# Attention regrouped into runs of eight products, and an auction step with its thresholds on VectorE

## The chip, the cores and the metric

The kernel runs on one core of one Trainium2 chip. The metric is the device time of one execution in microseconds (us). A core has a matrix engine (TensorE, PE in the profile, with its weight loads as PEld), a vector engine (VectorE, DVE), a scalar engine (ScalarE, ACT), GpSimd (POOL) and SyncE (SP), which in this kernel only issues transfers. Each engine works through its own instructions in the order in which they are written; they wait for one another through semaphores.

## The reference

Three parts follow one another: a sigmoid attention, a mixture of experts whose tokens are assigned greedily under a capacity, and a dense layer pair with a squared activation. Cut to what matters:

```
scores = q @ k.T / sqrt(64) - log(448)            # 4 batches, 12 heads, 448 x 64
x = sigmoid(scores) @ v                           # -> 1792 tokens x 768
logits = x @ w_gate                               # 1792 x 8 experts
for idx in argsort(-logits.flatten()):            # best (token, expert) first
    if token is free and expert has < 224 tokens: assign
h = relu(x[mask] @ w1[e]); y[mask] = h @ w2[e]     # per expert, 768 -> 1024 -> 768
r = relu(y @ w_in); out = (s * r * r + b) @ w_out  # 768 -> 2048 -> 768
```

## The kernel before

The program has a schedule written out by hand: what stands first in the source is issued first on its engine.

**Attention.** There are 24 pairs (4 batches b, 6 pairs of heads p). For a pair the scores come in four chunks of 112 keys (`NC = 4`). A score chunk is two products (tile psc, one head each, side by side on TensorE), followed by one sigmoid on ScalarE into attn. A value chunk is two products into pv, summed over the four chunks; then ScalarE copies pv to xT. In `scores_av(n, i, mid)` two score chunks of pair n = i + 1 alternate with two value chunks of pair i, so TensorE changes between score products and value products after every four products. psc has two buffers, pv two. The trace counts two records for each such product. Through the callback `mid` the gate's products are put between these groups: `gate` (logits of a batch, tile plg), `gate_copy`, `gate_turn` (to tokens by experts, tile pt), `gate_last` (the last pair of the last batch, which needs its xT). `prefs` on VectorE then ranks a batch's logits; `bracket`, in three stages during the last batch, finds the range for the first threshold.

Beside this, 32 blocks of the dense weights are converted from 64 bit to 32 bit (`convert`, on VectorE): craw is loaded, four VectorE instructions make co, and co is written to nw. `CONV[i]` says how many follow pair i. SyncE issues, in this order for pair i, vt of pair i + 2, rk and rq of pair i + 3, then the writes and loads of the conversions. `w_dma`, `w_high` and `w_low` prepare the first expert weights (the last on GpSimd here).

**Auction.** The assignment is found by a parallel search of ten steps. An array of 128 lines holds (chunk of tokens, expert), 112 tokens wide. A step claims with the present threshold (`choose`: VectorE aw, TensorE pa), takes out lost tokens (VectorE LM), counts at ten thresholds (six compares on VectorE, three sign passes on ScalarE, counted into cnt), sums the counts on TensorE (pb), and takes from them the new threshold (jd, into dv) and the factor for the next step size (jf, into cut). From the second step on, GpSimd makes the step sizes (dv) and thresholds (th) from dv, cut and least. In the same steps TensorE turns x to token rows (`rows_in`: four transposes into px for one of 24 rows), ScalarE copies px to xrow, and a transfer writes xrow to xs in HBM; `ROWS` says how many rows go with each step. The first four transfers are issued by ScalarE, the others by SyncE.

**Places and experts.** `places` turns the claims into row numbers idx: one-hot rows oh on VectorE, 32 small products on TensorE (pi), two copies and two sums. GpSimd then gathers the first expert's rows from xs; `keep_clock` puts idle products on TensorE meanwhile. The experts and the dense layers follow and fill the rest of the program.

Of the kernel before, what the change touches and what calls it, by code (L numbers as in the profile page):

```python
# [8 lines left out]
F32 = mybir.dt.float32  # L9
# [15 lines left out]
CP = 112  # L25
# [14 lines left out]
WARM = (9, 10)  # L40
ROWS = (2, 2, 2, 3, 3, 3, 2, 2, 2, 2)
SYNC = 4
SIGNS = 2
CONV = [1, 1, 2, 1, 2] * 4 + [1, 2, 1]
FULL = CAP - 0.5
# [16 lines left out]
def tile_kernel(ctx, tc, qT, kT, v, wg, w1, w2, wi, wo, s2, b2, cst, out):  # L62
# [55 lines left out]
    att = ExitStack()  # L118
    qk = att.enter_context(tc.tile_pool(name="qk", bufs=4))
    vp = att.enter_context(tc.tile_pool(name="vp", bufs=2))  # L120
    at = att.enter_context(tc.tile_pool(name="at", bufs=2))
    ps_s = att.enter_context(tc.tile_pool(name="ps_s", bufs=2, space=PSUM))
    ps_v = att.enter_context(tc.tile_pool(name="ps_v", bufs=2, space=PSUM))
    ps_l = att.enter_context(tc.tile_pool(name="ps_l", bufs=1, space=PSUM))
# [22 lines left out]
    def convert():  # L147
        if not coming:
            return
        i = coming.pop(0)  # L150
        r = craw.pop(i)
        lo, hi = r[:, :, 0], r[:, :, 1]
        b = cgp.tile([128, 768], I32, name="cb_", bufs=2)
        a = cgp.tile([128, 768], I32, name="co", bufs=3)
        V.tensor_scalar(a, hi, 3, 0x3FFFFFFF, op0=ALU.logical_shift_left, op1=ALU.bitwise_and)
        V.tensor_scalar(b, lo.bitcast(U32), 2.0 ** -29, None, op0=ALU.mult)
        V.scalar_tensor_tensor(a, hi, -(1 << 30), a, op0=ALU.bitwise_and, op1=ALU.bitwise_or)
        V.tensor_tensor(a, a, b, op=ALU.add)
        cout.append((i, a))
        cv_out(1)  # L160
        cv_in()
# [48 lines left out]
    def load_v(i):  # L210
        b, p = pairs[i]
        vt[i] = vp.tile([CP, NC, 128], F32, name="vt", bufs=4)
        nc.sync.dma_start(vt[i], v[b, p])
# [8 lines left out]

    def scores_av(n, i, mid):
        if n is not None:
            rq, rk = raw_qk.pop(n)
            attn[n] = at.tile([CP, 2, NC, S], F32, name="attn")
        if i is not None:
            a = attn.pop(i)
            pv = ps_v.tile([128, 512], F32, name="pv")
        for c2 in range(0, NC, 2):  # L230
            for c in (c2, c2 + 1):
                mid(c)
                if n is not None:
                    p = ps_s.tile([CP, 2, 512], F32, name="psc")
                    for j in range(2):
                        me = slice(j * D, (j + 1) * D)
                        T.matmul(p[:, j, :S], rk[me, c * CP:(c + 1) * CP], rq[me], start=True, stop=True)  # L237
                    A.activation(attn[n][:, :, c, :], p[:, :, :S], AF.Sigmoid, bias=nls[:CP],  # L238
                                 scale=1.0 / math.sqrt(D))
            for c in (c2, c2 + 1):  # L240
                if i is not None:
                    for j in range(2):
                        T.matmul(pv[j * 64:(j + 1) * 64, :S], vt[i][:, c, j * D:(j + 1) * D], a[:, j, c, :],  # L243
                                 start=(c == 0), stop=(c == NC - 1))
        if i is not None:
            b, p = pairs[i]
            xt = xT[:, p, b * S:(b + 1) * S]
            if i == len(pairs) - 1:
                A.copy(xt[:, :2 * CP], pv[:, :2 * CP])
                A.copy(xt[:, 2 * CP:], pv[:, 2 * CP:S])  # L250
            else:
                A.copy(xt, pv[:, :S])

    def gate(b, p0, p1, last):
        if p0 == 0:
            plg[b] = ps_l.tile([128, 512], F32, name="plg")
        for p in range(p0, p1):
            i = p % 4
            T.matmul(plg[b][i * 32:(i + 1) * 32, :S], wgs[:, p], xT[:, p, b * S:(b + 1) * S],
                     start=(p < 4), stop=(p + 4 >= last))  # L260
# [5 lines left out]
    def gate_turn(b, stop):  # L266
        lg = lgs.pop(b)
        pt = ps_l.tile([128, 512], F32, name="pt")
        pts[b] = pt[:CP, :NC * E].rearrange("p (c e) -> p c e", e=E)
# [20 lines left out]
    def bracket(stage):  # L290
# [4 lines left out]
        elif stage == 1:  # L295
            pm = ps_l.tile([128, 512], F32, name="plg")
            T.transpose(pm[:2, :CP], mm[:CP], ident[:CP, :CP])
# [3 lines left out]
        else:  # L301
            pr = ps_l.tile([128, 512], F32, name="plg")
            T.matmul(pr[:, :2], on[:2], dg, start=True, stop=True)
# [29 lines left out]
    load_qk(2)  # L333
    cv_in()
    cv_in()
    cv_in()
    scores_av(0, None, lambda c: None)
    nc.sync.dma_start(sb2[:, 0:1], s2.partition_broadcast(128))
# [13 lines left out]
    for i in range(N):  # L352
        b, p = pairs[i]
        if i + 2 < N:
            load_v(i + 2)
        if i + 3 < N:
            load_qk(i + 3)
        def mid(c):
            if b == B - 1 and p == 5:
                if c == 0:  # L360
                    gate(b, 0, 5, 5)
                elif c == 2:
                    gate_copy(b)
                elif c == 3:
                    gate_turn(b, False)
            elif p == 5 and c == 0:
                gate(b, 0, 4, 6)
            elif p == 0 and b and c == 1:
                gate(b - 1, 4, 6, 6)
            elif p == 0 and b and c == 3:  # L370
                gate_copy(b - 1)
            elif p == 1 and b and c == 0:
                gate_turn(b - 1, True)

        scores_av(i + 1 if i + 1 < N else None, i, mid)
        if p == 1 and b:
            prefs(b - 1)
        if b == B - 1 and 2 <= p <= 4:
            bracket(p - 2)
        if N - 6 <= i < N - 2:  # L380
# [4 lines left out]
        if i < N - 1:  # L385
            for _ in range(CONV[i]):
                convert()
    gate_last(B - 1)
    prefs(B - 1)
# [31 lines left out]

    got = rows_in(1)
    pl = ps_1.tile([128, CP], F32, name="pl")
# [15 lines left out]
    def auction(n, fill):  # L439
        for it in range(n):  # L440
            if fill and it == 0:
                pv = choose(dv[0], pw)
                V.tensor_copy(WT, pw)
            else:
                pv = choose(dv[0])
# [3 lines left out]
            if it or not fill:  # L449
                G.tensor_scalar(dv[0][:, 1:], dv[1][:, 1:], cut, least, op0=ALU.mult, op1=ALU.max)  # L450
                G.tensor_scalar(th, kvec, dv[0][:, 1:2], dv[0][:, 0:1], op0=ALU.mult, op1=ALU.add)
            V.scalar_tensor_tensor(LM, pv, -BIG, LT, op0=ALU.mult, op1=ALU.min)
# [17 lines left out]
            if fill:  # L470
                if it in AHEAD:
                    w_dma()
            dv.reverse()
            V.scalar_tensor_tensor(jd, pc[:, 1:], FULL, dv[1], op0=ALU.is_ge, op1=ALU.mult,
                                   accum_out=dv[0][:, 0:1])
            V.scalar_tensor_tensor(jf, pc, FULL, fvec, op0=ALU.is_ge, op1=ALU.mult, accum_out=cut)
        settle(choose(dv[0]))

# [358 lines left out]
```

## Time and profile before

| | us |
|---|---|
| three runs | 963.48, 968.11, 972.67 |
| median | 968.11 |
| the profiled execution | 965.9 |
| its span, first to last instruction | 964.1 |

The profiled execution lies 2.2 us below the median, and 1.8 us of its time lie around the span. TensorE is busy 97% of the span, VectorE 58%, ScalarE 46%, GpSimd 14%. The span can be read in four stretches: attention to about 180 us, the auction from there to about 217 us, places and the first gather to about 228 us, and the experts and dense layers from there to the end. TensorE's granted clock is full in the first and the last stretch and half of that in most of the auction.

### The profile page before, as it was taken

What the parts mean: (1) busy time and instruction counts of PE and PEld (TensorE: products, weight loads), DVE (VectorE), ACT (ScalarE), POOL (GpSimd) and SP (SyncE); (2) the same over time, 40 slices, a digit from 0 to 9 for tenths busy, and PEclk for the clock granted to TensorE, in tenths of its full rate; (3) what the DMA queues carried; (4) which work ended last, traced back from release to release, by engine and by line L of the source; (5) the groups of instructions that cost most, each with busy time, mean ns of one, the idle gap of its engine ahead of it and who ended that gap; (6) DMA issues with size and microseconds to landing.
All of it is one profiled execution on the core that took longest, in us unless ns stands there. A gap on an engine that the chain in (4) does not pass through costs nothing.

```text
span 964.1 us, 14094 instructions
## 1 busy us (share of the span) xinstructions
PE 937.4 (97%) x5277; PEld 782.4 (81%) x5277; DVE 563.9 (58%) x1015; ACT 443.8 (46%) x771; POOL 137.4 (14%) x136
## 2 busy tenths in 40 slices
PE   9999999778999999999999999999999999999997
PEld 3333333466899999999999999999999999999997
DVE  3565635764777774278677321877774278677320
ACT  5666666573564332266533223664332266433220
POOL 1000001223330000153100002430000152100001
PEclk9999999857999999999999999999999999999999
DMA  8999996272674434477443433774434476533411
GB/s 288 380 318 360 351 374 230 98 228 79 208 232 145 124 114 137 131 244 234 142 138 108 127 99 91 262 233 147 118 116 140 131 235 204 152 121 109 119 46 66
DMA packets 68456, 173.08 MB, mean 180 GB/s; under 512 B 7968, under 2 KB 24864, under 8 KB 68384
## 3 DMA queue, kind: packets, MB, share of 16 engines
q1 hardware_dynamic: 64256, 160.22, 51.5%
q0 software_dynamic: 2272, 11.01, 3.3%
q10 hardware_dynamic: 1856, 0.92, 0.3%
q8 instruction: 42, 0.69, 0.3%
q14 instruction: 30, 0.25, 0.1%
HBM read 148.52 MB, written 23.59 MB: 179 GB/s over the span
## 4 chain that ended last, share of the span: by engine, by line
PE 82%; DVE 6%; DMA 5%; issue 3%; ACT 2%; POOL 1%; SPq 1%; POOLq 0%; ACTq 0%; DVEq 0%
PE acc L642 9%; PE acc L708 8%; PE acc L710 8%; PE acc L709 8%; PE acc L759 8%; PE acc L761 8%; PE acc L760 8%; PE pv L243 7%; PE psc L237 7%; PE acc L643 5%; DVE wl L198 2%; DMA raw<-in_w_dram 2%; DMA rq<-in_qT_dram 2%; PE px L409 2%; ACT wh L187 1%
## 5 line engine op out<-in xcount | busy, mean ns | idle before, releaser
L187 ACT CAST wh<-raw 128x768 fp32r<-128x768 f32 (+1 forms) x240 | 209.2, 878 | 160.1 <-PE acc L761 133.8
L198 DVE TENSOR_TENSOR wl<-raw,wh 128x768 fp32r<-128x768 f32 (+1 forms) x198 | 210.5, 1068 | 104.9 <-ACT wh L187 104.9
L198 POOL TENSOR_TENSOR wl<-raw,wh 128x768 fp32r<-128x768 f32 (+1 forms) x42 | 92.1, 2201 | 433.4 <-ACT wh L187 285.2
L759 PE MATMUL acc<-wh,gt 128*128 128x384 f32 x448 | 149.9, 335 | 0.0
L760 PE MATMUL acc<-wl,gt 128*128 128x384 f32 x448 | 149.7, 334 | 0.0
L761 PE MATMUL acc<-wh,gt 128*128 128x384 f32 x448 | 149.6, 334 | 0.0
L708 PE MATMUL acc<-y,wh 128*128 128x448 f32 x384 | 141.4, 368 | 0.0
L710 PE MATMUL acc<-y,wl 128*128 128x448 f32 x384 | 140.6, 366 | 0.0
L709 PE MATMUL acc<-y,wh 128*128 128x448 f32 x384 | 140.6, 366 | 0.0
L642 PE MATMUL acc<-u,wh 128*128 128x448 f32 x384 | 121.7, 375 | 1.7 <-DVE u L666 1.5
L238 ACT ACTIVATE attn<-psc,nls 112x896 f32<-112x896 f32 x96 | 92.1, 1005 | 53.8 <-PE psc L237 53.8
L732 ACT ACTIVATE r<-acc 128x448 f32<-128x448 f32 x64 | 34.9, 545 | 150.9 <-PE acc L710 150.9
L643 PE MATMUL acc<-u,wl 128*128 128x224 f32 x384 | 101.5, 264 | 0.0
L642 PE MATMUL acc<-x,wh 128*128 128x448 f32 x288 | 95.3, 385 | 0.0
L237 PE MATMUL psc<-rq,rk 64*112 64x448 f32 x384 | 85.6, 561 | 1.1 <-ACT attn L238 0.6
L760 PEld LDWEIGHTS acc<-wl,gt 128*128 128x128 f32 x448 | 84.1, 188 | 0.0
L759 PEld LDWEIGHTS acc<-wh,gt 128*128 128x128 f32 x448 | 84.1, 188 | 0.0
L761 PEld LDWEIGHTS acc<-wh,gt 128*128 128x128 f32 x448 | 84.1, 188 | 0.0
L243 PE MATMUL pv<-attn,vt 112*64 112x448 f32 x384 | 82.8, 552 | 0.0
L643 PE MATMUL acc<-x,wl 128*128 128x224 f32 x288 | 77.2, 268 | 2.1 <-POOL wl L198 2.1
L733 DVE SCALAR_TENSOR_TENSOR r<-r,sb 128x448 f32<-128x448 f32 x64 | 43.8, 685 | 60.4 <-ACT r L732 60.3
L642 PEld LDWEIGHTS acc<-u,wh 128*128 128x128 f32 x384 | 72.0, 188 | 8.6 <-DVE u L666 3.3
(214 smaller groups left out, 1245.3 us busy)
## 6 DMA issues: line engine op xcount, KB each, us to landing
raw<-nw SPq DMA_DIRECT2D x128, 384.0 KB, 3.0
raw<-in_w_dram SPq DMA_DIRECT2D x64, 384.0 KB, 3.7
raw<-in_w_dram SPq DMA_DIRECT2D x48, 512.0 KB, 4.4
craw<-in_wi_dram SPq DMA_DIRECT2D x16, 768.0 KB, 7.6
nw<-co SPq DMA_DIRECT2D x32, 384.0 KB, 8.0
craw<-in_wo_dram SPq DMA_DIRECT2D x16, 768.0 KB, 6.9
rk<-in_kT_dram SPq DMA_DIRECT2D x24, 224.0 KB, 9.2
rq<-in_qT_dram SPq DMA_DIRECT2D x24, 224.0 KB, 8.4
```

The source lines that it names most:

```text
L187: A.copy(h[:, :k], raws[i][:, :k])
L198: eng.tensor_sub(lo[:, :k], r[:, :k], h[:, :k].bitcast(F32))
L237: T.matmul(p[:, j, :S], rk[me, c * CP:(c + 1) * CP], rq[me], start=True, stop=True)
L243: T.matmul(pv[j * 64:(j + 1) * 64, :S], vt[i][:, c, j * D:(j + 1) * D], a[:, j, c, :], start=(c == 0), stop=(c == NC - 1))
L642: T.matmul(p[:, :2 * CAP], wh[:, k], src[:, k].rearrange("p a s -> p (a s)"), start=(k == 0), stop=False)
L643: T.matmul(p[:, :CAP], wl[:, k], src[:, k, 0], start=False, stop=(k == n - 1))
L708: T.matmul(p, wh, src[:, k, 0], start=first, stop=False)
L709: T.matmul(p, wh, src[:, k, 1], start=False, stop=False)
L710: T.matmul(p, wl, src[:, k, 0], start=False, stop=last)
L759: T.matmul(ps[t][:, :DH], hi, wh[:, cols], start=(f == 0), stop=False)
L760: T.matmul(ps[t][:, :DH], hi, wl[:, cols], start=False, stop=False)
L761: T.matmul(ps[t][:, :DH], lo, wh[:, cols], start=False, stop=(f == KG - 1))
```

## The change

The change regroups the attention, spreads the rows evenly over the auction's steps, and changes order and engine of four instructions of an auction step.

- `scores_av` is replaced by `scores(n, c0, c1)` and `values(i)`. For pair i come the eight value products, then chunks 2 and 3 of the scores of pair i + 1 and chunks 0 and 1 of pair i + 2. psc has three buffers and pv one; gate, turn and bracket tiles share one bank ("small").
- The gate's products stand behind the group of score products of a pair. The last batch's `gate_turn` moves behind the last value products, directly ahead of `gate_last`. `bracket` and `prefs` come one pair earlier.
- rk and rq are loaded four pairs ahead (before: three), vt three pairs ahead (before: two), with one buffer more each, and rk and rq come ahead of vt. The last conversions come one pair earlier.
- `rows_in(3)` instead of `rows_in(1)` stands ahead of the auction, and each step takes two rows. That makes 23 rows; the 24th falls to `rest` in `places`.
- In a step, `choose` stands ahead of the factor `cut`, and the step sizes and thresholds are made on VectorE instead of GpSimd.

```diff
-ROWS = (2, 2, 2, 3, 3, 3, 2, 2, 2, 2)
+ROWS = (2, 2, 2, 2, 2, 2, 2, 2, 2, 2)
-CONV = [1, 1, 2, 1, 2] * 4 + [1, 2, 1]
+CONV = [1, 1, 2, 1, 2] * 4 + [2, 2, 0]
...
-    qk = att.enter_context(tc.tile_pool(name="qk", bufs=4))
+    qk = att.enter_context(tc.tile_pool(name="qk", bufs=5))
...
-    ps_s = att.enter_context(tc.tile_pool(name="ps_s", bufs=2, space=PSUM))
-    ps_v = att.enter_context(tc.tile_pool(name="ps_v", bufs=2, space=PSUM))
+    ps_s = att.enter_context(tc.tile_pool(name="ps_s", bufs=3, space=PSUM))
+    ps_v = att.enter_context(tc.tile_pool(name="ps_v", bufs=1, space=PSUM))
...
-        b = cgp.tile([128, 768], I32, name="cb_", bufs=2)
+        b = cgp.tile([128, 768], I32, name="cb_", bufs=1)
...
-        vt[i] = vp.tile([CP, NC, 128], F32, name="vt", bufs=4)
+        vt[i] = vp.tile([CP, NC, 128], F32, name="vt", bufs=5)
...
+    def scores(n, c0, c1):
+        if n >= len(pairs):
+            return
+        if c0 == 0:
             attn[n] = at.tile([CP, 2, NC, S], F32, name="attn")
+        rq, rk = raw_qk[n]
+        for c in range(c0, c1):
+            p = ps_s.tile([CP, 2, 512], F32, name="psc")
+            for j in range(2):
+                me = slice(j * D, (j + 1) * D)
+                T.matmul(p[:, j, :S], rk[me, c * CP:(c + 1) * CP], rq[me], start=True, stop=True)
+            A.activation(attn[n][:, :, c, :], p[:, :, :S], AF.Sigmoid, bias=nls[:CP], scale=1.0 / math.sqrt(D))
...
+    def values(i):
+        a, v = attn.pop(i), vt.pop(i)
+        pv = ps_v.tile([128, 512], F32, name="pv")
+        for c in range(NC):
+            for j in range(2):
+                T.matmul(pv[j * 64:(j + 1) * 64, :S], v[:, c, j * D:(j + 1) * D], a[:, j, c, :],
+                         start=(c == 0), stop=(c == NC - 1))
...
     load_v(1)
     load_qk(2)
     cv_in()
+    load_qk(3)
+    load_v(2)
     cv_in()
     cv_in()
-    scores_av(0, None, lambda c: None)
+    scores(0, 0, NC)
+    scores(1, 0, 2)
...
-        if i + 2 < N:
-            load_v(i + 2)
+        if i + 4 < N:
+            load_qk(i + 4)
         if i + 3 < N:
-            load_qk(i + 3)
...
-        scores_av(i + 1 if i + 1 < N else None, i, mid)
-        if p == 1 and b:
+            load_v(i + 3)
+        values(i)
+        scores(i + 1, 2, NC)
+        scores(i + 2, 0, 2)
+        if p == 0 and b:
+            gate_turn(b - 1, True)
             prefs(b - 1)
-        if b == B - 1 and 2 <= p <= 4:
-            bracket(p - 2)
+        elif p == 4:
+            gate(b, 0, 4 if b < B - 1 else 5, 6 if b < B - 1 else 5)
+            if b == B - 1:
+                gate_copy(b)
+        elif p == 5 and b < B - 1:
+            gate(b, 4, 6, 6)
+            gate_copy(b)
+        if b == B - 1 and 1 <= p <= 3:
+            bracket(p - 1)
...
+    gate_turn(B - 1, False)
     gate_last(B - 1)
...
-    got = rows_in(1)
+    got = rows_in(3)
...
-            else:
+            elif it == 0:
                 pv = choose(dv[0])
...
             if it or not fill:
-                G.tensor_scalar(dv[0][:, 1:], dv[1][:, 1:], cut, least, op0=ALU.mult, op1=ALU.max)
-                G.tensor_scalar(th, kvec, dv[0][:, 1:2], dv[0][:, 0:1], op0=ALU.mult, op1=ALU.add)
+                V.tensor_scalar(dv[0][:, 1:], dv[1][:, 1:], cut, least, op0=ALU.mult, op1=ALU.max)
+                V.tensor_scalar(th, kvec, dv[0][:, 1:2], dv[0][:, 0:1], op0=ALU.mult, op1=ALU.add)
...
                                    accum_out=dv[0][:, 0:1])
+            pv = choose(dv[0])
             V.scalar_tensor_tensor(jf, pc, FULL, fvec, op0=ALU.is_ge, op1=ALU.mult, accum_out=cut)
-        settle(choose(dv[0]))
+        settle(pv)
```

How this moves the instructions shows on three engines. First TensorE at the start of the attention; psc are score products, pv value products, and x4 is the number of products in a row. Before:

```order
L237 MATMUL psc<-rq,rk 112x448 x12
L243 MATMUL pv<-attn,vt 64x448 x4
L237 MATMUL psc<-rq,rk 112x448 x4
L243 MATMUL pv<-attn,vt 64x448 x4
L237 MATMUL psc<-rq,rk 112x448 x4
L243 MATMUL pv<-attn,vt 64x448 x4
```

After the change, in the same place:

```order
L233 MATMUL psc<-rq,rk 112x448 x12
L243 MATMUL pv<-attn,vt 64x448 x8
L233 MATMUL psc<-rq,rk 112x448 x8
L243 MATMUL pv<-attn,vt 64x448 x8
L233 MATMUL psc<-rq,rk 112x448 x8
```

The groups are twice as long and half as many.

Next VectorE in the auction, from the counts of a step to the first compare of the next; in brackets the engines waited for. Before:

```order
L474 SCALAR_TENSOR_TENSOR jd,dv_95<-pb,dv_94 128x9 [waits PE_49]
L476 SCALAR_TENSOR_TENSOR jf,cut<-pb,ct 128x10
L431 SCALAR_TENSOR_TENSOR aw<-LT,dv_95,WT 128x112 [waits DVE_49]
L452 SCALAR_TENSOR_TENSOR LM<-pa,LT 128x112 [waits PE_49,Activation_49]
L464 SCALAR_TENSOR_TENSOR junk_111,cnt<-LM,th 128x112 [waits DVE_49,Pool_49]
```

After the change:

```order
L470 SCALAR_TENSOR_TENSOR jd,dv_95<-pb,dv_94 128x9 [waits PE_49]
L427 SCALAR_TENSOR_TENSOR aw<-LT,dv_95,WT 128x112 [waits DVE_49]
L473 SCALAR_TENSOR_TENSOR jf,cut<-pb,ct 128x10
L446 TENSOR_SCALAR dv_95<-dv_94,cut,least 128x8 [waits DVE_49]
L447 TENSOR_SCALAR th<-ct,dv_95 128x8 [waits DVE_49,Activation_49]
L448 SCALAR_TENSOR_TENSOR LM<-pa,LT 128x112 [waits PE_49]
L460 SCALAR_TENSOR_TENSOR junk_111,cnt<-LM,th 128x112 [waits DVE_49]
```

aw has moved ahead of jf, and two instructions of GpSimd stand between jf and LM; the compare no longer waits for GpSimd.

Last TensorE in places, between the products that check the counts (pb) and the first one-hot product (pi). Before:

```order
L509 MATMUL pi<-P,cb 112x128
L483 LDWEIGHTS cb
L483 MATMUL pb<-cnt_102,cb 128x1
L486 MATMUL pb<-on,ok 1x1
L525 LDWEIGHTS oh
L525 MATMUL pi<-R,oh 128x16
```

After the change:

```order
L506 MATMUL pi<-P,cb 112x128
L480 LDWEIGHTS cb
L480 MATMUL pb<-cnt_102,cb 128x1
L483 MATMUL pb<-on,ok 1x1
L405 MATMUL px<-ident,xT 112x128 x4
L522 LDWEIGHTS oh
L522 MATMUL pi<-R,oh 128x16
```

The four transposes of the last row stand ahead of the 32 one-hot products.

## Rows read from the trace of the kernel before

**Rows 1.** The page's chain of work that ended last, shares by engine.
```profile
PE 82%; DVE 6%; DMA 5%; issue 3%; ACT 2%; POOL 1%; SPq 1%; POOLq 0%; ACTq 0%; DVEq 0%
```
**Rows 2.** Busy time by stretch: stretch, length, then PE, PEld, DVE, ACT, POOL, clock, DMA.
```profile
260.00:964.00 704.00, 696.49 (x4044) 666.80 (x4043) 416.66 (x615) 288.95 (x516) 103.30 (x75) 1.00 0.47 148
```
**Rows 3.** Timeline of TensorE in mid-attention: start, length, line, tiles, records in a row.
```profile
112.26 1.76 PE L237 MATMUL psc<-rq,rk 64*112 64x448 f32 x8
113.95 1.72 PE L243 MATMUL pv<-attn,vt 112*64 112x448 f32 x8
115.60 1.76 PE L237 MATMUL psc<-rq,rk 64*112 64x448 f32 x8
```
**Rows 4.** Timeline of TensorE's weight loads in the first of these groups.
```profile
112.73 0.18 PEld L237 LDWEIGHTS psc<-rq,rk 64*112 64x112 f32 x2 [0.20 <-issue]
113.10 0.18 PEld L237 LDWEIGHTS psc<-rq,rk 64*112 64x112 f32 x2 [0.20 <-issue]
```
**Rows 5.** Timeline of ScalarE there; in brackets the idle time before, and its releaser.
```profile
113.31 1.91 ACT L238 ACTIVATE attn<-psc,nls 112x896 f32<-112x896 f32 x2 [1.38 <-PE psc L237]
115.72 0.53 ACT L252 COPY xT<-pv 128x448 f32<-128x448 f32 x1 [0.50 <-PE pv L243]
```
**Rows 6.** Timeline of TensorE early in the attention.
```profile
22.96 1.76 PE L237 MATMUL psc<-rq,rk 64*112 64x448 f32 x8 [0.53 <-DMA rq<-in_qT_dram]
```
**Rows 7.** The page's GB/s in 40 slices of 24.1 us.
```profile
GB/s 288 380 318 360 351 374 230 98 228 79 208 232 145 124 114 137 131 244 234 142 138 108 127 99 91 262 233 147 118 116 140 131 235 204 152 121 109 119 46 66
```
**Rows 8.** Waits up to 182 us: total us, times, longest.
```profile
DVE L L280 <- PE pt L271: 23.4, 3, 10.4
```
**Rows 9.** Timeline of TensorE at the end of the attention.
```profile
173.29 1.69 PE L259 MATMUL plg<-xT,wgs 128*32 128x448 f32 x10 [0.77 <-DVE mm L304]
...
179.62 0.95 PE L276 MATMUL pt<-wgs,xT 128*112 128x8 f32 x8 [0.45 <-ACT xT L249]
...
183.43 0.31 PE L427 MATMUL pb<-ident,Wp 112*128 112x112 f32 x1 [2.26 <-DVE Wp L287]
```
**Rows 10.** Timeline of all engines in one auction step with two rows.
```profile
210.10 0.17 DVE L474 SCALAR_TENSOR_TENSOR jd<-pb,dv 128x9 f32<-128x9 f32 x1 [0.38 <-PE pb L469]
...
210.31 0.34 DVE L431 SCALAR_TENSOR_TENSOR aw<-LT,dv,WT 128x112 bf16<-128x112 f32 x1
210.46 0.45 POOL L450 TENSOR_SCALAR dv<-dv,cut,least 128x8 f32<-128x8 f32 x1 [2.08 <-DVE jf L476]
...
211.01 0.35 POOL L451 TENSOR_SCALAR th<-ct,dv 128x8 f32<-128x8 f32 x1
211.06 0.28 DVE L452 SCALAR_TENSOR_TENSOR LM<-pa,LT 128x112 f32<-128x112 f32 x1 [0.41 <-PE pa L433]
...
212.61 0.19 ACT L456 ACTIVATION_READ_ACCUMULATOR junk<-LM,th 128x1 bf16 x1
...
213.09 0.17 DVE L474 SCALAR_TENSOR_TENSOR jd<-pb,dv 128x9 f32<-128x9 f32 x1 [0.38 <-PE pb L469]
```
**Rows 11.** Timeline of VectorE, two ends of steps, the second with three rows.
```profile
200.32 0.17 DVE L474 SCALAR_TENSOR_TENSOR jd<-pb,dv 128x9 f32<-128x9 f32 x1 [1.21 <-PE pb L469]
...
204.13 0.17 DVE L474 SCALAR_TENSOR_TENSOR jd<-pb,dv 128x9 f32<-128x9 f32 x1 [1.21 <-PE pb L469]
```
**Rows 12.** Timeline of TensorE in that step: the transposes of three rows.
```profile
201.22 2.81 PE L409 MATMUL px<-ident,xT 128*112 128x128 f32 x12
```
**Rows 13.** Timeline of ScalarE in the first two steps: copy and issue of a row.
```profile
187.03 0.59 ACT L416 COPY xrow<-px 112x512 f32<-112x512 f32 x1 [0.38 <-ACT xrow L416]
187.64 0.31 ACTq L417 DMA_DIRECT2D xs<-xrow  x1
```
**Rows 14.** Timeline of all engines in places.
```profile
219.87 2.64 PE L525 MATMUL pi<-R,oh 112*128 112x16 bf16 x32
...
223.14 1.18 POOL L539 DMA_INDIRECT xr<-xs,idx  x1 [4.65 <-DVE idx L529]
```
**Rows 15.** The writes of rows to xs, from issue to landing.
```profile
DMA to landing us min/median/max: 2.4/3.2/4.8
```

More of the change, by code (lines that the diff above doesn't have):

```diff
@@ L221, in load_qk @@
         raw_qk[i] = (rq, rk)
-    def scores_av(n, i, mid):
-        if n is not None:
-            rq, rk = raw_qk.pop(n)
+    def scores(n, c0, c1):
+        if n >= len(pairs):
+            return
+        if c0 == 0:
             attn[n] = at.tile([CP, 2, NC, S], F32, name="attn")
[L227 to L250, printed above, removed]
-            else:
-                A.copy(xt, pv[:, :S])
@@ new lines, in scores @@
+        rq, rk = raw_qk[n]
[5 more added lines that the diff above has]
+            A.activation(attn[n][:, :, c, :], p[:, :, :S], AF.Sigmoid, bias=nls[:CP], scale=1.0 / math.sqrt(D))
+        if c1 == NC:
+            raw_qk.pop(n)
+    def values(i):
[5 more added lines that the diff above has]
+                         start=(c == 0), stop=(c == NC - 1))
+        b, p = pairs[i]
+        xt = xT[:, p, b * S:(b + 1) * S]
+        if i == len(pairs) - 1:
+            A.copy(xt[:, :2 * CP], pv[:, :2 * CP])
+            A.copy(xt[:, 2 * CP:], pv[:, 2 * CP:S])
+        else:
+            A.copy(xt, pv[:, :S])
@@ L254, in gate @@
     def gate(b, p0, p1, last):
         if p0 == 0:
-            plg[b] = ps_l.tile([128, 512], F32, name="plg")
+            plg[b] = ps_l.tile([128, 512], F32, name="small")
         for p in range(p0, p1):
@@ L267, in gate_turn @@
         lg = lgs.pop(b)
-        pt = ps_l.tile([128, 512], F32, name="pt")
+        pt = ps_l.tile([128, 512], F32, name="small")
         pts[b] = pt[:CP, :NC * E].rearrange("p (c e) -> p c e", e=E)
@@ L295, in bracket @@
         elif stage == 1:
-            pm = ps_l.tile([128, 512], F32, name="plg")
+            pm = ps_l.tile([128, 512], F32, name="small")
             T.transpose(pm[:2, :CP], mm[:CP], ident[:CP, :CP])
@@ L301, in bracket @@
         else:
-            pr = ps_l.tile([128, 512], F32, name="plg")
+            pr = ps_l.tile([128, 512], F32, name="small")
             T.matmul(pr[:, :2], on[:2], dg, start=True, stop=True)
@@ L353, in tile_kernel @@
         b, p = pairs[i]
-        if i + 2 < N:
-            load_v(i + 2)
+        if i + 4 < N:
+            load_qk(i + 4)
         if i + 3 < N:
-            load_qk(i + 3)
[L358 to L373, printed above, removed]
-        scores_av(i + 1 if i + 1 < N else None, i, mid)
-        if p == 1 and b:
-            prefs(b - 1)
-        if b == B - 1 and 2 <= p <= 4:
-            bracket(p - 2)
+            load_v(i + 3)
[4 more added lines that the diff above has]
+            gate_turn(b - 1, True)
+            prefs(b - 1)
+        elif p == 4:
[7 more added lines that the diff above has]
+            bracket(p - 1)
         if N - 6 <= i < N - 2:
@@ L443, in auction @@
                 V.tensor_copy(WT, pw)
-            else:
+            elif it == 0:
                 pv = choose(dv[0])
```

## Prediction

> **What bounds the kernel now.** I read the chain of work that ended last first: 82% of it is TensorE [rows 1]. The table by stretch says where: from 260 us on, TensorE is busy 696.49 of 704 us at the full clock [rows 2]. No edit touches that stretch, so it keeps its length and starts earlier or later as a whole. What counts is when the first expert's rows are gathered, and so the length of the attention, the auction and places.
>
> In the attention TensorE sets the pace too. Eight records of score products, eight of value products and the next score group follow each other without a wait: 112.26, 113.95, 115.60 us [rows 3]. One score group and one value group last 3.34 us. The reader is to see that this isn't all streaming: inside a group the weight loads come 0.37 us apart (112.73, 113.10) [rows 4]. A group of four products has four such beats, since two products run side by side and each makes two records, so eight beats are 2.96 to 3.0 us. The remaining 0.34 to 0.38 us is spent at the two changes between score and value products: the first beat of the score group is 0.47 us (112.26 to 112.73), the second 0.37. The border between the two chunks of a group lies between beats two and three and costs nothing extra. ScalarE waits for TensorE there (1.38 us before the sigmoids [rows 5]), so it isn't the bound.
>
> In the auction no engine is full; a step is a round of short instructions, from one jd to the next: 2.99 us with two rows of x [rows 10], 3.81 us with three (200.32 to 204.13 [rows 11]). There the twelve transposes, 2.81 us [rows 12], hold up the counts: VectorE waits 1.21 us for TensorE, against 0.38 us with two rows.
>
> **Attention.** After the first twelve products the trace has 48 score groups and 48 value groups (45 and three that a gate splits); in the new order it is 23 and 24. That takes away 24 pairs of changes at 0.35 us: 8.4 us. Three waits of TensorE go with it. rq was late once by 0.53 us [rows 6]; the loads for this pair are now issued ahead of two conversions. The gate of the last batch waited 0.77 us for VectorE's copy of the bracket [rows 9]; that copy now comes a pair earlier. The last gate products waited 0.45 us for ScalarE's copies of xT [rows 9]; now gate_turn stands between. That is 1.75 us, and 10.1 us in all. Bounds: 8.4 us if other waits take the place of the three, and 10.9 us at 0.38 us a change pair. What is late next: the conversions on VectorE, ahead of the last batch's prefs (a rival below).
>
> The third score bank covers the longer groups: the first sigmoid starts 1.05 us into a group (112.26 to 113.31) and one takes 0.955 us, half of 1.91 [rows 5], so its bank is free at 2.0 us, and the fourth chunk wants it after six beats, at 2.3 us. The single pv bank costs nothing: the copy is 0.53 us [rows 5], and a score group of over 3 us lies before the next value products.
>
> **Ahead of the auction.** Two more rows are transposed, copied and sent. The eight transposes cost TensorE 0.94 us at the full clock (half of what twelve take per piece at half clock [rows 12]) inside a wait of 2.26 us for VectorE [rows 9], so nothing there. On ScalarE each row is a copy of 0.59 us and an issue of 0.31 us [rows 13], 0.95 us with the gaps, and it can't start on the next sign pass before. Two more rows are 1.9 us; about 1.3 us of the 2.26 us wait is left as cover once the transposes are done. I take 0.6 us lost in the first step, between 0 (all covered) and 1.9.
>
> **The steps.** Three steps go from three rows to two: 3 x 0.82 = 2.5 us gained. The reordering on VectorE: aw starts 0.21 us after jd (210.10, 210.31) because it needs jd's sum, and it will need it in the new order too; so pa comes at the same time, or at best 0.09 us earlier, by jf's place. LM starts 0.96 us after jd, having waited 0.41 us for pa [rows 10]. Into that wait now go jf and the two instructions from GpSimd. The trace shows no such instruction of eight elements on VectorE in a step; the nearest row is jd, nine elements, 0.17 us [rows 10]; the farthest is the same work on GpSimd, 0.45 and 0.35 us [rows 10]. Three at 0.17 us are 0.51 us against 0.41: LM 0.10 us late. Three with GpSimd's prices are 0.97 us: 0.56 us late. In return the compares and sign passes lose their wait for th. A step ends with ScalarE's last pass (212.61 + 0.19 = 212.80) [rows 10], which follows LM. I take 0.05 us, near the lower row, nine times: 0.5 us lost; bounds -0.8 and +5 us. GpSimd being free of this work gains nothing: it has nothing else to do there.
>
> **Places.** The 24th row falls behind the auction. Its four transposes (2.81 / 3 = 0.94 us at half clock [rows 12]) stand ahead of the one-hot products, which take 2.64 us and directly release what the gather needs [rows 14]: idx 0.94 us later. The gather also reads xs, so it waits for the row: transposed by 219.87 + 0.94 = 220.81, copied by about 221.45, landed 2.4 to 4.8 us after its issue [rows 15], at 223.9 to 226.3 us; the gather, so far at 223.14 [rows 14], is ready at 224.08. The loss is 0.94 to 3.1 us. This write is alone in its queue, so I go near the low end: 1.2 us. No other row's write is late by this, since the others are issued as before or earlier.
>
> **Sum.** -10.1 + 0.6 - 2.5 + 0.5 + 1.2 = -10.3 us. The profiled execution of 965.9 us would be 955.6. It lies 2.2 us below the median of the runs shown, so for a median I forecast 957.8 us. A measurement of this kernel tells about 1% from no change, 9.7 us; the forecast is just beyond it.
>
> **Rivals.** *Transfers hold the attention.* The conversions need their loads, and the last prefs stands behind them on VectorE. The first seven slices of 24.1 us move 55.5 MB at a mean of 329 GB/s [rows 7]; in ten us less it would have to be 350. Against: VectorE waited 23.4 us at three prefs for TensorE [rows 8], so conversions are ahead, and single slices reach 374 and 380 GB/s [rows 7]. For: others stay at 318 and 351. At a rate half way, 340 GB/s, half the attention's gain goes: 963 us. The Trainium skill, in "Perfetto Trace Analysis", section Roofline, gives 358 GB/s as a core's share and says that a core alone can draw some 120% of it; the slices agree that more than 358 is drawn, and by either figure 55.5 MB fit into 158 us.
>
> *A change costs nothing and the lost time belongs to each chunk.* Then 8.4 us stay: 966.2 us. Against it is that the border of two chunks inside a group shows no gap.
>
> *Score groups wait for ScalarE: slower than before.* Eight score products in a row need four banks and there are three. If the first sigmoid comes 0.3 us later into the group than now, the fourth chunk waits, and a group goes at the pace of four sigmoids, 4 x 0.955 = 3.82 us in place of 3.17. That is 0.65 us in 22 groups, 14.3 us: 972.1 us. For it: it needs only the xT copy to slip. Against: ScalarE has 4.4 us of work in a round of 6.3. The Trainium skill has this as a rule, "TensorEngine Tiling (Array Packing)", section PSUM Bottleneck: tiling speeds up TensorE and not the emptying of PSUM, which can become the limit. By that rule the time would be this rival's; rows 5, with ScalarE idle 1.38 us, speak for the forecast so far.
>
> *VectorE's new instructions cost what GpSimd's did.* 0.5 us more in nine steps: 962.3 us.
>
> *More is gained.* The extra rows are covered and the last row lands in time: 955 us, or less with 0.38 us a pair of changes.
>
> **How the numbers follow.** Forecast 0.67 (954.5 to 961.5 us, by the bounds of the first step, places and the changes, and the runs' own spread); transfers 0.12; GpSimd's prices 0.05; cost per chunk 0.05; ScalarE 0.04; more gained 0.07. The range of 952.5 to 964.5 us leaves out the cost per chunk, ScalarE and the far ends of the others, under 0.2. Faster by over 1% is below 958.4 us: some 0.6 of the forecast and all of "more gained" with a little of the rest, 0.52. Slower by over 1%, above 977.8 us, needs ScalarE or the transfers at their worst, 0.03. Within 1%: 0.45.
>
> **What would show it.** Right: score and value groups twice as long, 3.2 us each, 6.3 us a round, TensorE never waiting for attn or rq; the last gate products about 10 us earlier; ten steps near 3.0 us with the first about 0.6 us longer than now; LM about 1.0 to 1.1 us after jd; the gather some 10 us earlier than 223.14. Wrong: beats of 0.47 us inside a long group; idle TensorE before the fourth score chunk; prefs late behind a conversion; a gather released by xs well after idx. What would upset it most is a wait that comes back in every one of the 22 rounds: 0.1 us there is 2.2 us of the sum.

## The result, and the profile after

| | us |
|---|---|
| kernel before, median of 10 runs | 966.62 (963.48 to 972.67) |
| changed kernel, median of 10 runs | 958.43 (956.84 to 960.81) |
| ratio, with its 95% interval | 0.9912 (0.9890 to 0.9934) |
| profiled execution after, and its span | 958.63, 956.8 |

The change made the kernel 8.2 us faster by the medians and 7.3 us by the two profiled executions; the forecast was 10.3. That is 0.9%: within the 1% that one measurement tells from no change, and below no change by its interval.

The chain of work that ended last, shares by engine, answers to [rows 1], and the table by stretch (stretch, length, busy time of PE, PEld, DVE, ACT, POOL, clock, DMA) to [rows 2]. From the page and from the table:

```profile
PE 83%; DVE 5%; DMA 4%; issue 3%; ACT 3%; POOL 1%; POOLq 0%; ACTq 0%; DVEq 0%; SPq 0%
```
```profile
252.40:956.40 704.00, 696.34 (x4046) 666.99 (x4044) 416.76 (x615) 289.11 (x516) 103.30 (x75) 1.00 0.47 148
10.00:160.00 150.00, 150.00 (x779) 57.49 (x779) 90.80 (x139) 97.49 (x117) 3.85 (x9) 1.00 0.96 347
```

The last 704 us are what they were, 696.34 us of TensorE, shifted as a whole. From 10 to 160 us, in the attention, TensorE is now busy 150 of 150 us, so no wait for rq as in [rows 6] is left there.

Timeline of TensorE in mid-attention, then its weight loads and ScalarE in the same group; these answer to [rows 3 to 5]:

```profile
101.86 3.27 PE L233 MATMUL psc<-rq,rk 64*112 64x448 f32 x16
105.06 3.23 PE L243 MATMUL pv<-attn,vt 112*64 112x448 f32 x16
108.22 3.26 PE L233 MATMUL psc<-rq,rk 64*112 64x448 f32 x16
```
```profile
101.86 0.27 PEld L233 LDWEIGHTS psc<-rq,rk 64*112 64x112 f32 x4 [0.70 <-issue]
102.33 0.18 PEld L233 LDWEIGHTS psc<-rq,rk 64*112 64x112 f32 x2 [0.20 <-issue]
102.71 0.18 PEld L233 LDWEIGHTS psc<-rq,rk 64*112 64x112 f32 x2 [0.20 <-issue]
```
```profile
102.92 3.71 ACT L234 ACTIVATE attn<-psc,nls 112x896 f32<-112x896 f32 x4 [0.41 <-PE psc L233]
```

A round of one score and one value group takes 6.36 us (101.86 to 108.22). Two rounds of half the size took 2 x 3.34 = 6.68 us before. The long first beat (101.86 to 102.33, 0.47 us) comes once in sixteen records; the beats behind it are 0.38 us.

Timeline of TensorE at the end of the attention, answering to [rows 9]:

```profile
163.86 1.69 PE L258 MATMUL small<-xT,wgs 128*32 128x448 f32 x10
...
169.45 0.93 PE L275 MATMUL small<-wgs,xT 128*112 128x8 f32 x8
...
172.98 0.32 PE L423 MATMUL pb<-ident,Wp 112*128 112x112 f32 x1 [1.15 <-DVE Wp L286]
```

The first two groups of gate products (163.86 and 169.45 us) follow what stands ahead of them without a wait; in [rows 9] they waited 0.77 and 0.45 us. The last gate products start at 169.45 us in place of 179.62, 10.17 us earlier.

Timeline of all engines in one auction step, from jd to the next jd, answering to [rows 10]:

```profile
196.40 0.17 DVE L470 SCALAR_TENSOR_TENSOR jd<-pb,dv 128x9 f32<-128x9 f32 x1 [0.45 <-PE pb L465]
...
196.61 0.34 DVE L427 SCALAR_TENSOR_TENSOR aw<-LT,dv,WT 128x112 bf16<-128x112 f32 x1
196.86 0.16 DVE L473 SCALAR_TENSOR_TENSOR jf<-pb,ct 128x10 f32<-128x10 f32 x1
...
197.07 0.29 DVE L446 TENSOR_SCALAR dv<-dv,cut,least 128x8 f32<-128x8 f32 x1
...
197.47 0.29 DVE L447 TENSOR_SCALAR th<-ct,dv 128x8 f32<-128x8 f32 x1
197.67 0.27 DVE L448 SCALAR_TENSOR_TENSOR LM<-pa,LT 128x112 f32<-128x112 f32 x1
...
199.69 0.17 DVE L470 SCALAR_TENSOR_TENSOR jd<-pb,dv 128x9 f32<-128x9 f32 x1 [0.45 <-PE pb L465]
```

A step now takes 3.29 us in place of 2.99 with the same two rows, and LM starts 1.27 us after jd in place of 0.96. VectorE goes from aw to LM without idle time that waits for pa; the path runs through its own instructions.

Timeline of all engines in places, answering to [rows 14]:

```profile
210.15 1.10 PE L405 MATMUL px<-ident,xT 128*112 128x128 f32 x4
...
211.04 1.90 PE L522 MATMUL pi<-R,oh 112*128 112x16 bf16 x32
...
211.90 0.30 SPq L413 DMA_DIRECT2D xs<-xrow  x1
...
213.09 0.24 DVE L526 SCALAR_TENSOR_TENSOR idx<-pi,ia 128x8 int32<-128x8 f32 x2 [0.64 <-ACT ia L525]
215.29 1.16 POOL L536 DMA_INDIRECT xr<-xs,idx  x1 [6.61 <-issue]
```

The gather starts 2.2 us after the first idx and 3.4 us after the last row's write was issued. The trace has this write landing 2.3 us after its issue, at about 214.2 us, just under the 2.4 to 4.8 us of [rows 15]; what holds the gather for the remaining 1.1 us is shown by no row. Before, the gather started 0.5 us after idx (223.14 us in [rows 14]):

```profile
222.66 0.24 DVE L529 SCALAR_TENSOR_TENSOR idx<-pi,ia 128x8 int32<-128x8 f32 x2 [0.49 <-ACT ia L528]
```

The account of the two profiled executions, by the prediction's terms (from the timelines; minus is earlier than before):

| stretch | forecast | measured |
|---|---|---|
| attention, to the last gate products | -10.1 | -10.17 |
| from there to the end of the first step | +0.6 | +0.42 |
| nine steps | -2.5 + 0.5 | -0.05 |
| last step to the gather | +1.2 | +1.95 |
| at the gather | -10.3 | -7.85 |
| from there to the end | 0 | +0.5 |

Two terms carry the difference: the reordering on VectorE and the last row.

### The profile page after: what moved, and what is told of

Read it like the earlier page. It is cut to its first block, busy times and chain, and to the rows that moved or that the text cites. A ratio compares the mean times of both kernels' runs of the same rounds, so it can differ in the third digit from the quotient of the medians.

```text
span 956.8 us, 14074 instructions
## 1 busy us (share of the span) xinstructions
PE 930.1 (97%) x5277; PEld 786.2 (82%) x5277; DVE 570.0 (60%) x1033; ACT 440.9 (46%) x771; POOL 129.9 (14%) x118
## 4 chain that ended last, share of the span: by engine, by line
PE 83%; DVE 5%; DMA 4%; issue 3%; ACT 3%; POOL 1%; POOLq 0%; ACTq 0%; DVEq 0%; SPq 0%
PE acc L639 10%; PE acc L705 8%; PE acc L707 8%; PE acc L706 8%; PE psc L233 8%; PE acc L758 8%; PE acc L757 8%; PE acc L756 8%; PE pv L243 8%; PE acc L640 5%; DMA raw<-in_w_dram 3%; DVE wl L198 2%; ACT junk L452 1%; ACT wh L187 1%; DMA xr<-xs,idx 1%
## 5 line engine op out<-in xcount | busy, mean ns | idle before, releaser
L234 ACT ACTIVATE attn<-psc,nls 112x896 f32<-112x896 f32 x96 | 88.9, 1008 | 14.2 <-PE psc L233 14.2
L233 PE MATMUL psc<-rq,rk 64*112 64x448 f32 x384 | 79.3, 552 | 0.0
L243 PE MATMUL pv<-attn,vt 112*64 112x448 f32 x384 | 77.5, 545 | 0.0
```

The lines of the kernel that those rows point to most:

```text
L243: T.matmul(pv[j * 64:(j + 1) * 64, :S], v[:, c, j * D:(j + 1) * D], a[:, j, c, :], start=(c == 0), stop=(c == NC - 1))
```

## The experiments

Times are medians; ratios are to the kernel before, on the same chip.

### Order and engine of the auction step apart

`a_gpsimd_factor_first` takes the changed kernel and puts both back:

```diff
-                V.tensor_scalar(dv[0][:, 1:], dv[1][:, 1:], cut, least, op0=ALU.mult, op1=ALU.max)
-                V.tensor_scalar(th, kvec, dv[0][:, 1:2], dv[0][:, 0:1], op0=ALU.mult, op1=ALU.add)
+                G.tensor_scalar(dv[0][:, 1:], dv[1][:, 1:], cut, least, op0=ALU.mult, op1=ALU.max)
+                G.tensor_scalar(th, kvec, dv[0][:, 1:2], dv[0][:, 0:1], op0=ALU.mult, op1=ALU.add)
...
-            pv = choose(dv[0])
             V.scalar_tensor_tensor(jf, pc, FULL, fvec, op0=ALU.is_ge, op1=ALU.mult, accum_out=cut)
+            pv = choose(dv[0])
```

`b_gpsimd_claims_first` has only the first half of this diff, `c_vector_factor_first` only the second.

> The changed kernel with the auction step of the kernel before: factor ahead of the claims, step sizes and thresholds on GpSimd; two rows a step and all else as changed. Theory 1 (the new order on VectorE makes LM late: 1.27 us after jd instead of 0.96, and a step 3.29 us instead of 2.99): LM back at 0.96 us, steps of 3.0 us, nine steps 2.6 us shorter, about 955.8 us. Rival (the steps got longer for another reason, such as the transposes or the row copies): steps stay at 3.29 us, 958.4 us.

> The changed kernel with claims ahead of the factor, but step sizes and thresholds on GpSimd. Theory 1a (the order is what costs: jf ends 0.25 us later, and all that needs cut is late by as much): GpSimd's thresholds end about 1.6 us after jd, the compares start there, the step is 3.2 to 3.35 us, about 958 us. Theory 1b (the engine is what costs): LM at 0.96 us and steps of 3.0 us, 955.8 us.

> The changed kernel with the factor ahead of the claims, step sizes and thresholds on VectorE. Theory 1a (the order costs): the two instructions follow aw without waiting for jf, LM at 1.05 us after jd, steps of 3.05 to 3.1 us, about 956.5 us. Theory 1b (the engine costs): steps stay at 3.29 us, 958.4 us.

| thresholds on | first in a step | one step, us | LM after jd, us | time, us | ratio (95%) |
|---|---|---|---|---|---|
| GpSimd | factor (a) | 2.99 | 0.96 | 955.38 | 0.9910 (0.9894 to 0.9927) |
| VectorE | factor (c) | 3.07 | 1.05 | 955.42 | 0.9905 (0.9889 to 0.9922) |
| GpSimd | claims (b) | 3.13 | 0.96 | 956.73 | 0.9922 (0.9905 to 0.9938) |
| VectorE | claims (changed kernel) | 3.28 | 1.27 | 958.43 | 0.9912 (0.9890 to 0.9934), another chip |

The step is the distance from the first jd to the tenth, by nine (in c from the first to the ninth, by eight). Claims first costs 0.21 us a step on VectorE and 0.15 with GpSimd; VectorE for GpSimd costs 0.08 us with the factor first and 0.15 with the claims first. Together they are 0.30 us, nine times 2.7 us. The whole times tell less: on one chip b lies 1.3 us above a and c, but the changed kernel ran on another, and its ratio lies between theirs. So the 2.7 us rest on the steps, and on the gather, which starts at 212.57 us in a and at 215.29 in the changed kernel, with the last gate products at the same time (169.47 and 169.45 us). Timeline of VectorE in a step of c, with the four instructions in the other order:

```profile
194.03 0.17 DVE L470 SCALAR_TENSOR_TENSOR jd<-pb,dv 128x9 f32<-128x9 f32 x1 [0.45 <-PE pb L465]
194.12 0.16 DVE L472 SCALAR_TENSOR_TENSOR jf<-pb,ct 128x10 f32<-128x10 f32 x1
194.23 0.33 DVE L427 SCALAR_TENSOR_TENSOR aw<-LT,dv,WT 128x112 bf16<-128x112 f32 x1
194.49 0.29 DVE L446 TENSOR_SCALAR dv<-dv,cut,least 128x8 f32<-128x8 f32 x1
194.88 0.29 DVE L447 TENSOR_SCALAR th<-ct,dv 128x8 f32<-128x8 f32 x1
195.08 0.27 DVE L448 SCALAR_TENSOR_TENSOR LM<-pa,LT 128x112 f32<-128x112 f32 x1
```

aw starts 0.20 or 0.21 us behind jd in either order, since it needs jd's sum. In c, jf fits into that gap and costs nothing, and dv starts 0.46 us after jd. In the changed kernel nothing stands in the gap, jf comes behind aw, and dv has to wait for its sum: 0.67 us after jd. That is the 0.21 us. With GpSimd and the claims first (b), LM is on time, but the compares wait for GpSimd and start 1.61 us after jd (195.56 to 197.17), as this piece of a step shows:

```profile
195.56 0.17 DVE L470 SCALAR_TENSOR_TENSOR jd<-pb,dv 128x9 f32<-128x9 f32 x1 [0.26 <-PE pb L465]
...
196.52 0.27 DVE L448 SCALAR_TENSOR_TENSOR LM<-pa,LT 128x112 f32<-128x112 f32 x1 [0.33 <-PE pa L429]
196.79 0.35 POOL L447 TENSOR_SCALAR th<-ct,dv 128x8 f32<-128x8 f32 x1
...
197.17 0.28 DVE L460 SCALAR_TENSOR_TENSOR junk<-LM,th 128x112 bf16<-128x112 f32 x1 [0.38 <-POOL th L447]
```

### The last row in the last step

```diff
-ROWS = (2, 2, 2, 2, 2, 2, 2, 2, 2, 2)
+ROWS = (2, 2, 2, 2, 2, 2, 2, 2, 2, 3)
```

> The changed kernel with three rows in the last step, so that none is left for places. Theory 2 (the first gather waits for the late row's write to xs): the last step 0.5 us longer, the gather 0.3 us after idx instead of 2.2, about 957.0 us. Rival (something else holds GpSimd): the gather stays 2.2 us after idx, and the time is 958.9 us.

957.11 us, 0.9926 (0.9902 to 0.9949). Timeline in its places:

```profile
215.28 0.24 DVE L526 SCALAR_TENSOR_TENSOR idx<-pi,ia 128x8 int32<-128x8 f32 x2 [0.49 <-ACT ia L525]
...
215.75 1.16 POOL L536 DMA_INDIRECT xr<-xs,idx  x1 [4.72 <-DVE idx L526]
```

The gather starts 0.5 us after idx and idx releases it; in a, b and c, which keep the late row, it starts 2.2 us after. So in the changed kernel it was the late row that held it. The write of this row accounts for the time up to its landing; the 1.1 us behind that go away with it, and their cause is not shown. The whole time shows less: the step with three rows costs part of it (VectorE waits 0.97 us for the counts there in place of 0.45), and in this profiled execution the last prefs came late behind a conversion, so that the auction began 1.7 us later. The time alone doesn't tell d from the changed kernel; the release does.

### The changes between score and value products

`e_groups_of_four` keeps loads, banks and the places of the gate, and splits each value group (`values` gets a range of chunks and keeps pv from its first call to its second):

```diff
-        values(i)
+        values(i, 0, 2)
         scores(i + 1, 2, NC)
+        values(i, 2, NC)
         scores(i + 2, 0, 2)
```

> The attention of the changed kernel, with its loads, its three score banks and its one value bank, but a value group split in two: four value products, chunks 2 and 3 of the next pair, four value products, chunks 0 and 1 of the pair after. That is 23 pairs of changes between score and value products more. The theory, that a pair of changes costs 0.35 us: a round of 6.70 us in place of 6.36, the gate's last products near 177.5 us in place of 169.45, and 8.1 us more than the changed kernel, about 966.5 us beside a kernel before of 966 us. The rival, that the gain came from the loads, the banks or the gate's place and a change costs nothing: rounds of 6.36 us and 958.4 us.

965.54 us, 0.9990 (0.9977 to 1.0004): 7.5 us more than the changed kernel by the two ratios. Timeline of TensorE:

```profile
104.23 1.76 PE L233 MATMUL psc<-rq,rk 64*112 64x448 f32 x8
105.92 1.72 PE L244 MATMUL pv<-attn,vt 112*64 112x448 f32 x8
...
110.92 1.76 PE L233 MATMUL psc<-rq,rk 64*112 64x448 f32 x8
```

6.69 us for two small rounds (104.23 to 110.92). From the first value products to the last it takes 162.24 us (10.31 to 172.55) and the changed kernel 154.64 (10.84 to 165.48). Behind the last pair no score products are left to split a group by, so 22 pairs of changes differ, not the expected 23: 7.6 / 22 = 0.345 us a pair. Neither kernel waits on TensorE in that stretch.

### One half of the change without the other

`f_attention_only` is the changed kernel with a's diff, `rows_in(1)` and the old ROWS. `g_auction_only` is the kernel before with the new order and engine, `rows_in(3)` and the new ROWS.

> The attention of the changed kernel with the auction, the rows of each step and the places of the kernel before. If the account by stretches adds up (attention 10.2 us gained, first step 0.7 lost, the steps together nothing, the gather 1.7 lost): 10.2 us less than the kernel before, 956 us beside 966, the first step 2.60 us, idx released to the gather within 0.5 us, and some 2.4 us faster than the changed kernel. The rival, that a later stretch takes some of it back (the clock, or weights that land too late for the first expert): 958 us or more.

> The attention of the kernel before, with the three rows ahead of the auction, the two rows in each step, the order and the engine of the changed kernel. By the account of the stretches: slower than the kernel before by 0.7 us in the first step, nothing in the steps (2.5 gained, 2.7 lost), 1.7 us at the gather: 2.4 us, 968.5 us beside 966. Steps of 3.29 us. The rival, that the order of the auction only costs together with the new attention: 966 us or less.

f: 954.84 us, 0.9883 (0.9854 to 0.9912), 11.3 us faster than before (8.5 to 14.1 by the interval). g: 969.79 us, 1.0035 (1.0015 to 1.0056), 3.6 us slower (1.4 to 5.4). The halves add up within these intervals: -11.3 + 3.6 = -7.7, and the whole measured -8.2 on its chip. So the attention is the whole gain, and what was done to the auction is, taken together, a loss. f takes no part of it back later. g lost 1.2 us more than expected, 0.85 of it in its first step: 4.14 us from aw to jd in place of the 3.29 of the changed kernel. The three rows start later there, as the timelines of ScalarE show, first the changed kernel, then g:

```profile
172.11 0.58 ACT L412 COPY xrow<-px 112x512 f32<-112x512 f32 x1
```
```profile
183.60 0.58 ACT L416 COPY xrow<-px 112x512 f32<-112x512 f32 x1 [1.05 <-DVE Wp L287]
```

In g, as in the kernel before, the first copy waits for VectorE's Wp; in the changed kernel it doesn't. The copy doesn't read Wp. That xrow lies where a tile of the attention lay that VectorE used last, and that the new pool sizes moved it, is my reading; it was not tried.

### Two score banks

```diff
-    ps_s = att.enter_context(tc.tile_pool(name="ps_s", bufs=3, space=PSUM))
+    ps_s = att.enter_context(tc.tile_pool(name="ps_s", bufs=2, space=PSUM))
```

> The changed kernel with two score banks in place of three. In the changed kernel's trace the first sigmoid of a group ends 2.0 us after the group's first product and the third chunk is due at 1.55 us. If the third bank is what covers the longer groups: the third chunk waits some 0.4 us and the fourth some 0.2 us for a bank, 0.6 us in each of 22 rounds, 13 us, about 971.5 us beside a kernel before of 966, and rounds of 6.95 us. The rival, that the longer groups needed no third bank: rounds of 6.36 us and 958.4 us.

974.80 us, 1.0085 (1.0055 to 1.0116). Timeline of TensorE:

```profile
111.64 1.76 PE L233 MATMUL psc<-rq,rk 64*112 64x448 f32 x8
113.76 1.91 PE L233 MATMUL psc<-rq,rk 64*112 64x448 f32 x8 [0.36 <-ACT attn L234]
115.59 0.60 PE L243 MATMUL pv<-attn,vt 112*64 112x448 f32 x2
```

The score group takes 3.95 us (111.64 to 115.59) in place of 3.20, with a wait for ScalarE in the middle; 0.75 us in 22 rounds is 16.5 us, and 16.4 were measured (974.80 less 958.43, on two chips). With two banks the regrouping would have been a loss.

### The best of these, and the clock behind the gather

`i_gpsimd_and_row` is a with d's diff. `j_more_idle_products` is i with 16 idle products during the first gather:

```diff
-WARM = (9, 10)
+WARM = (9, 16)
```

> The changed kernel with the factor ahead of the claims, step sizes and thresholds on GpSimd, as the kernel before has them, and the last row in the last step. If both losses add: steps of 2.99 us, the last of them 3.8 us with three rows; the gather within 0.5 us of idx instead of 2.2; 955.4 (the same without the row) + 0.8 - 1.8 = 954.4 us beside a kernel before of 964.4, so 0.989 of it. The rival, that the time of the gather hides behind the clock's rise or the first expert's weights: 955.4 us, 0.991 or more.

> The kernel with the factor ahead of the claims, thresholds on GpSimd and the last row in the last step, with 16 idle products on TensorE during the first gather in place of 10. In the trace with 10 the granted clock rose to 1.00 two us after they had ended (0.79 in 212 to 214 us, 1.00 in 214 to 216), TensorE was idle 2.69 us, and the first transposes ran at 0.57. If it is the idle time that loses the clock again: the transposes take 1.3 us in place of 2.47, the first products 0.38 in place of 0.74, some 1.5 us in all, 953.3 us where 10 products gave 954.8 (0.9865 of before). The rival, that the clock falls for another reason: the transposes stay at 2.4 us and the time at 954.8.

i: 954.83 us, 0.9881 (0.9859 to 0.9903). j: 953.67 us, 0.9875 (0.9840 to 0.9911). i's steps are 2.99 us, its gather starts 0.5 us after idx. TensorE's first work on the gathered rows, first of i, then of j:

```profile
216.28 2.47 PE L631 MATMUL acc<-ident,xr 128*128 128x128 f32 x12 [2.69 <-DMA xr<-xs,idx]
```
```profile
216.89 1.70 PE L631 MATMUL acc<-ident,xr 128*128 128x128 f32 x12 [0.75 <-DMA xr<-xs,idx]
```

In j the transposes find the full clock: 1.70 us in place of 2.47, and the first product comes 2.1 us behind the rows (216.89 to 218.99) in place of 2.45. The expected 1.3 us for the transposes isn't reached, and by the intervals i, j and f can't be told apart. All three have a lower ratio than the changed kernel's 0.9912. The intervals overlap with its own; but i's four times, 953.86 to 956.80 us, all lie below the changed kernel's ten, from 956.84 up, on chips where the kernel before has nearly the same median (966.17 and 966.62).

## Why the prediction was right or wrong

**Attention: right, in size and cause.** Forecast 10.1 us, measured 10.17. The price of 0.35 us for a pair of changes, read from two beats of [rows 3, 4], was 0.345 us when the changes alone were put back (e). The three waits are gone and none took their place: TensorE is busy without a break from 10 to 160 us. That the sum fits to 0.1 us is partly luck. Two waits for ScalarE among the first twelve products, of 0.35 and 0.21 us, went as well, and the prediction didn't count them. Timeline of TensorE before, the first of the two:

```profile
6.72 1.91 PE L237 MATMUL psc<-rq,rk 64*112 64x448 f32 x8 [0.35 <-ACT attn L238]
```

Against that, the first score product came 0.61 us later in the execution after (5.22 us in place of 4.61), as it did in g with the old attention. And g has no wait for rq, so the 0.53 us of [rows 6] belong to one execution and not to the kernel. From the first value products to the last gate products it is 168.94 us before and 158.61 after.

**The third bank covers the longer groups: right.** The rival "score groups wait for ScalarE" is real, but one bank away: without the third bank it costs 16.4 us, against the 14.3 that the prediction gave it.

**Transfers: the rival did not come in the changed kernel's trace, but it is near.** TensorE never stands idle for a load there, and in total 22.9 us of waiting for TensorE are left at VectorE's first three prefs against 23.4 in [rows 8]. At the last prefs the lead is small: VectorE waited 2.05 us for TensorE there before, 0.41 us after, and not at all in a and j. In d it came late, the sign of being wrong that the prediction named: a conversion had waited 1.42 us for a transfer (it began at 154.29 us), the last conversion took 6.0 us in place of 4.4, and the last prefs stood behind it. Timeline of VectorE, first the changed kernel, then d:

```profile
170.42 0.19 DVE L279 COPY L<-small 112x32 f32<-112x32 f32 x1 [0.41 <-PE small L275]
```
```profile
170.78 2.45 DVE L158 CUSTOM_DVE_ANT_0 co<-co,cb__1341 128x1536 uint16<-128x1536 uint16 x1
173.16 0.18 DVE L279 COPY L<-small 112x32 f32<-112x32 f32 x1
```

**The first step: near.** +0.42 us against +0.6, inside the bounds of 0 and 1.9. The step was longer by 0.69 us through the rows on ScalarE; 0.27 us came back ahead of it. g shows that a copy which waits for VectorE makes it 1.5 us.

**The steps: the term that was mis-sized.** "I take 0.05 us, near the lower row, nine times: 0.5 us lost". It was 0.30 us, 2.7 in all, and with it the 2.5 us gained from three-row steps were gone. The price was made from jd's busy time, 0.17 us, three times. Two things were wrong with that. dv and th are 0.29 us each. And what counts in a chain is the distance from start to start, 0.40 us from dv to th, since th needs dv: from dv's start to LM's it is 0.60 us (197.07 to 197.67), where the sum had 0.34. The row for the first was in the trace: the bracket makes th once on VectorE, outside the steps, where the prediction didn't look for it. Timeline of VectorE before, at the end of the bracket:

```profile
175.48 0.29 DVE L313 TENSOR_SCALAR th<-ct,dv 128x8 f32<-128x8 f32 x1
```

The order entered the sum only as jf's 0.17 us in the wait for pa, with the sentence that pa comes at the same time. It does: in b LM starts 0.96 us after jd, as before. But ahead of aw jf stood in a gap that was free; behind aw it moves dv and th back by 0.21 us. c shows this, and LM 1.27 us after jd lies outside the 1.0 to 1.1 that the prediction named. The return that the prediction set against it, compares that no longer wait for th, did not come: from LM to the next jd it is 2.02 us (197.67 to 199.69), and 2.03 before, so LM's delay reaches the step in full. Against its own bounds (up to +5 us) the value was inside; the choice of the nearest row was the error, not the range.

**Places: the lower end was too low.** +1.95 us against +1.2, inside 0.94 to 3.1. The mechanism was another: the transposes cost idx only 0.23 us, because the one-hot products ran in 1.90 us behind them in place of 2.64 [rows 14]. As far as the times show, VectorE's one-hot rows set the pace of these products: the last oh ended 0.33 us ahead of the last product before (222.18 us) and 0.49 us after (212.45 us), so most of the transposes fall into that time. The rest, 1.72 us, is the wait for the late row (d).

**After the gather.** The prediction let the rest of the program shift as a whole. The two profiled executions differ by 0.5 us there, and none of it lies ahead of the first product, which came 7.88 us earlier (230.64 and 222.76 us) where the gather came 7.85 us earlier. The first transposes began even 8.65 us earlier, but the rest of them waited 0.56 us for the second half of the rows, in place of 0.26, and ran with TensorE's granted clock at 0.50, where it was 0.80 from 228 to 230 us before. From the first product to the end it is 733.5 us before and 734.0 after. The twelve profiled executions, of kernels that don't differ from there on, take 731.5 to 734.9 us, so 0.5 us needs no cause in the change.

## What to carry to other kernels

Price an instruction that enters a chain by the distance from start to start of dependent instructions, taken from the same instruction wherever the trace has it, not by the busy time of a similar one. Where an engine waits for its own last result, that gap is free for independent work: an order that empties the gap and puts the work behind it pays for it in full. And when a change has parts, build each part alone: here the attention was worth 11.3 us and the auction's part cost 3.6.

## What was not expected of the hardware

A change between the two kinds of attention products, which divide TensorE in two different ways (64 rows by 112 columns and 112 by 64), costs 0.17 us on average, with nothing waited for. The Trainium skill, "TensorEngine Tiling (Array Packing)", section Key Properties, states that changing the tiling mode drains TensorE; the long beat at each group's start, 0.47 us against 0.38, is in line with that, but no run here changes the mode and nothing else.

VectorE is slower beside GpSimd. The same compare of the last prefs, first in the changed kernel, where GpSimd makes wl from 170.16 to 171.97 us, then in d, where it had ended:

```profile
170.64 1.61 DVE L283 TENSOR_TENSOR ge<-L 112x256 f32<-112x256 f32 x1
```
```profile
173.37 0.42 DVE L283 TENSOR_TENSOR ge<-L 112x256 f32<-112x256 f32 x1
```

1.61 us against 0.42, on the path to the first step. In the ten other traces it takes 1.60 to 1.88 us, each time beside a wl. A small instruction shows it too: the bracket's th, 0.29 us before and in d, takes 1.66 us in the changed kernel (161.27 us), where a wl runs from 161.07 to 162.91. That GpSimd's wl is the cause is read from these coincidences; no run moved it alone.

TensorE's clock, in the table by stretch of i and then of j (columns as above):

```profile
214.00:216.00 2.00, 0.00 (x0) 0.00 (x0) 0.00 (x0) 0.00 (x0) 0.00 (x0) 1.00 0.55 154
216.00:218.00 2.00, 1.72 (x9) 1.65 (x10) 0.25 (x1) 0.76 (x2) 0.00 (x0) 0.57 0.01 4
```
```profile
214.00:216.00 2.00, 2.00 (x8) 0.91 (x7) 0.00 (x0) 0.00 (x0) 0.00 (x0) 0.83 0.77 246
216.00:218.00 2.00, 1.12 (x9) 0.77 (x9) 0.00 (x0) 0.48 (x1) 0.00 (x0) 1.00 0.04 13
```

With ten idle products the granted clock had risen to 1.00 (2.4 GHz) when TensorE had nothing to do, and fell to 0.57 on average, half speed for most of it, as the transposes ran; with sixteen it was 1.00 when they came and stayed there.
